# Query blocks for the score mix: the GpSimd queue issues whole second blocks three steps ahead, the SyncE queue takes the rest

## The chip, the cores and the metric

One core of a Trainium2 chip runs the whole program. The metric is the device time of one execution in microseconds (us); three runs of the kernel before gave 610.6, 612.25 and 614.14 us, so the median is 612.25 us. Five engines work side by side, each through its own instruction queue in order: TensorE (PE for its matmuls, PEld for the weight loads that go ahead of them), VectorE (DVE), ScalarE (ACT), GpSimd (POOL) and SyncE (SP). A DMA is issued by an instruction in the queue of SP, ACT or POOL, and lands later.

## The reference, cut to what matters

```python
scores = scale * q @ k^T                              # batch 2, heads 12, seq 448, head_dim 64
scores = einsum('bhij,hg->bgij', scores, w_pre)       # heads mixed before the softmax
attn   = softmax(scores)                              # with max subtracted and 1e-9 added to the sum
attn   = einsum('bhij,hg->bgij', attn, w_post)        # heads mixed after it
x      = (attn @ v) as [896, 768]
x      = ELU(x @ w1i) @ w1o                           # d_ff 2048
out    = silu(x @ w2i) @ w2o                          # d_ff 2048
```

## The kernel before, in words

The kernel has two parts. The first 165 us or so are the attention; after that come the two dense layers, in which TensorE runs one matmul behind the other.

The 896 query rows (2 batches of 448) are cut in two ways. For the scores they lie in seven tiles of 128 rows (`QTILES`, built from `CUTS`), and `qk_pair` makes the scores of one pair of heads of one tile; `qk_evac` copies them to an SBUF tile `s` with queries on the partitions. For the mix over heads the kernel needs heads on the partitions instead. So the queries are also cut in 90 blocks of 10 (`BI`), 45 for each batch, and a DMA moves each block from the `s` tile to the buffer `blk`: 10 queries x 12 heads make 120 rows of 448 scores. This DMA, line 167 in `move`, is what the change is about.

A step `s` (`NB` = 45 of them) works on two blocks, the first block `c = 0` and the second block `c = 1`. `blkb` holds three steps' blocks (`NBUF = 3`, slot `s % NBUF`). In a step:

- `premix(s)` (line 202) multiplies both blocks with `w_pre`: eight weight loads and eight matmuls, four for the first block and then four for the second.
- `rmax` (DVE, line 208), `exps` (ACT, line 220) and `recip` (DVE lines 228 and 229, then POOL line 233, which writes `krn`) make the softmax of step `s`.
- `postmix(s - 1)` (line 245) applies `w_post` and the softmax's divisor for the step before; `post_evac` (ACT line 133, DVE line 135) copies the result out.
- On the steps in `AV_AT` TensorE also multiplies with `v` (line 273), on those in `QK_AT` it makes a pair of heads of the next score tile (line 149). Tiles 2 to 6 are complete after steps 6, 16, 22, 28 and 34.
- From step 16 on the first weight chunks of the dense layers are loaded, scaled and split in between.

A block whose ten queries lie in one score tile in an even spacing is one DMA (one piece); a block that lies on an edge of a tile is two or three pieces. `BLOCKS[seq[2 * s + c]]` lists the pieces of block `c` of step `s`. Pieces of a first block that lie in the earlier tile are issued one step sooner (`early`).

`pooled(s, c)` decides the queue: POOL issues the second blocks of steps 3 to 31 (`POOLED = (3, 32)`), SP all others. `relayout(s, True)` issues what POOL has of step `s`, `relayout(s)` what SP has. `AHEAD = 2`: both are called two steps ahead, POOL's at the top of `step`, SP's near its end. In SP's queue loads from HBM stand between the blocks: queries, keys, values and weights. In POOL's queue the order through the steps is therefore: block of step `s + 2`, `krn` of step `s`, block of step `s + 3`, `krn` of step `s + 1`, and so on. The order of the whole program is written out by hand (`manual_schedule`); each instruction waits on semaphores for what it reads and for the buffer that it overwrites.

Of the kernel before, what the change touches and what calls it, by code (L numbers as in the profile page):

```python
# [30 lines left out]
NBUF = 3  # L31
NE = 3
LEAD = 5
POOLED = (3, 32)
TURN = (29, 35, 41)
LATE = (35, 37, 41)
KO = (0, 2, 4, 1, 3, 5)
AHEAD = 2
# [19 lines left out]
def spread():  # L58

    tiles, blocks = [], {}  # L60
    for T, segs in enumerate(CUTS):
        of = [None] * P
        for b, q, n, whole, left, right in segs:
            k = -(-q // BI)
            for j, aps in [(k - 1, left)] + [(k + x, a) for x, a in enumerate(whole)] + [(k + n, right)]:
                i = q % BI if aps is left else 0
                for r, d, m in aps:
                    blocks.setdefault((b, j), []).append((T, r, d, m, i))
                    for x in range(m):
                        of[r + d * x] = (b, j * BI + i + x)  # L70
                    i += m
        tiles.append((of, [x[0] for x in segs]))
    return tiles, blocks


QTILES, BLOCKS = spread()
# [3 lines left out]
def attn_moe_moe(ctx: ExitStack, tc: tile.TileContext, q, k, v, w_pre, w_post, w1i, w1o, w2i, w2o, out):  # L80
# [81 lines left out]
    seq = [(b, n) for b in range(B) for n in range(KB)]  # L162
    NB = len(seq) // 2

    def move(s, c, piece):
        T, r, d, m, i = piece
        (nc.gpsimd if pooled(s, c) else nc.sync).dma_start(blkb[4 + H * i:4 + H * (i + m), s % NBUF, c], smap[T][r:r + d * (m - 1) + 1:d])

    def pooled(s, c):
        return c == 1 and POOLED[0] <= s < POOLED[1]  # L170

    def early(n):
        x = BLOCKS[seq[n]]
        return [y for y in x if n % 2 == 0 and y[0] < x[-1][0]]

    def relayout(s, pool=False):

        if s >= NB:
            return
        for c in range(2):  # L180
            if pooled(s, c) != pool:
                continue
            gone = early(2 * s + c)
            for piece in BLOCKS[seq[2 * s + c]]:
                if piece not in gone:
                    move(s, c, piece)
        if s + 1 < NB and not pool:
            for piece in early(2 * s + 2):
                move(s + 1, 0, piece)
# [6 lines left out]
    def premix(s):  # L196
        tags = (("pre1", "pre2"), ("av", "pre0"), ("qk1", "pre0"))[s % 2 + (s % 2 and s > NB - 9)]
        pre[s] = [ps.tile([P, S], F32, name=f"pre{s}_{r}", tag=tags[r], bufs=1) for r in range(2)]
        for c in range(2):
            for r in range(2):  # L200
                o = slice(HS * r, HS * r + (HS if r == 0 else BW))
                nc.tensor.matmul(pre[s][r][HS * c:HS * c + HS], kpre[o], blkb[o, s % NBUF, c], start=True, stop=True, tile_position=(HS * r, HS * c))  # L202

    def rmax(s):
        n = prow(s)
        nmx[s] = ap_.tile([P, 2], F32, name=f"nmx{s}", tag="nmx", bufs=3)
        for r in range(2):
            nc.vector.tensor_reduce(nmx[s][:n, r:r + 1], pre[s][r][:n], axis=AX.X, op=ALU.max, negate=True)  # L208
            if r == 0 and s - 1 in LATE:
                recip(s - 1)  # L210

    def exps(s, between=None):
        n = prow(s)
        pexp[s] = []
        sums[s] = ap_.tile([P, 2], F32, name=f"sum{s}", tag="sum", bufs=3)
        for r in range(2):
            if r and between:
                between()
            t = ap_.tile([P, S], F32, name=f"pe{s}_{r}", tag="pe", bufs=4)
            nc.scalar.activation(t[:n], pre[s][r][:n], AF.Exp, bias=nmx[s][:n, r:r + 1], scale=1.0, accum_out=sums[s][:n, r:r + 1])  # L220
            pexp[s].append(t)
        del pre[s], nmx[s]

    def recip(s):

        n = prow(s)
        z = sums.pop(s)
        nc.vector.tensor_scalar(z[:n], z[:n], 1e-9, None, op0=ALU.add)
        nc.vector.reciprocal(z[:n], z[:n])  # L229
        kr[s] = []  # L230
        for r in range(2):
            t = ap_.tile([P, H, 5], F32, name=f"krn{s}_{r}", tag="krn", bufs=4)
            nc.gpsimd.tensor_scalar(t[:n], kps[:n], z[:n, r:r + 1], None, op0=ALU.mult)  # L233
            kr[s].append(t)
# [3 lines left out]
    def postmix(s):  # L238

        w = pst[s] = [x.rearrange("p (r c) -> p r c", r=2) for x in pbank]  # L240
        for r, m in [(0, m) for m in range(6)] + [(0, 6), (1, 6)] + [(1, m) for m in range(6)]:
            u, j = r if m == 6 else m % 2, m // 2
            for c in range(2):
                o = slice(HS * c, HS * c + BW)
                nc.tensor.matmul(w[c][HS * u:HS * u + HS, r, j * BW:(j + 1) * BW], pexp[s][r][o, m * HS:(m + 1) * HS], kr[s][r][o].rearrange("p h i -> p (h i)"), start=True, stop=True, tile_position=(HS * c, HS * u))  # L245
        del pexp[s], kr[s]
# [4 lines left out]
    def post_evac(s):  # L251
        for c, w in enumerate(pst.pop(s)):
            b, n = seq[2 * s + c]
            T, n = 4 * b + n // 12, n % 12
            if T not in amap:
                amap[T] = ap_.tile([P, 4 * H, TI], F32, name=f"a{T}", tag="a", bufs=2)
            o = amap[T][:NV, :, n * BI:(n + 1) * BI].rearrange("p x (r i) -> p r x i", r=2)
            evac((nc.scalar, nc.vector)[c], o, w[:NV].rearrange("p r (x i) -> p r x i", i=5))
# [70 lines left out]
    def at(d, step, f):  # L329
        d.setdefault(int(step), []).append(f)  # L330
# [20 lines left out]
    def run(d, s):  # L351
        for f in d.get(s, []):
            f()

    def step(s):
        relayout(s + AHEAD, True)
        if s < NB:
            premix(s)
        if s - 1 in LATE:
            rmax(s)  # L360
        run(X_AT, s)
        run(QK_AT, s)
        run(F_AT, s)
        if 0 <= s - 1 < NB:
            postmix(s - 1)
        if s < NB:
            if s - 1 not in LATE:
                rmax(s)
            exps(s, (lambda: post_evac(s - 1)) if s in TURN else None)
        two = s in X_AT  # L370
        if two:
            run(B_AT, s)
            if s < NB:
                recip(s)
            av_evac()
            av_split()
            run(A_AT, s)
        qk_evac(0)
        qk_evac(1)
        if 0 <= s - 1 < NB and s not in TURN:  # L380
            post_evac(s - 1)
        if not two:
            run(B_AT, s)
            if s < NB and s not in LATE:
                recip(s)
        relayout(s + AHEAD)
        run(D_AT, s)
        run(M_AT, s)
# [616 lines left out]
    for n in range(O1 + 8, I2):  # L1005
# [4 lines left out]
        if po:  # L1010
            c = chunks[n][2]
# [122 lines left out]
    while n < NCH:  # L1134
        c, k = chunks[n][2:]
# [95 lines left out]
```

## Time and profile before

| | |
|---|---|
| median of three runs | 612.25 us (610.6 to 614.14) |
| the profiled execution | 610.48 us |
| its span (first to last instruction) | 608.7 us |
| granted TensorE clock | 0.999 of full speed |
| PE busy | 592.4 us, 97% of the span |
| DVE busy | 452.6 us, 74% |
| ACT busy | 373.0 us, 61% |
| POOL busy | 83.9 us, 14%, all in the first 175 us |
| `blk<-s` DMAs | 69 issued by SP, 35 by POOL |

"Busy" is counted by engine over the whole span. The chain of waits is the work that ended last, followed back from the last instruction to what released it each time. A number in square brackets behind an instruction is the time for which its engine stood idle before it, with what ended the wait.

### The profile page before, as it was taken

What the parts mean: (1) busy time and instruction counts of PE and PEld (TensorE: products, weight loads), DVE (VectorE), ACT (ScalarE), POOL (GpSimd) and SP (SyncE); (2) the same over time, 40 slices, a digit from 0 to 9 for tenths busy, and PEclk for the clock granted to TensorE, in tenths of its full rate; (3) what the DMA queues carried; (4) which work ended last, traced back from release to release, by engine and by line L of the source; (5) the groups of instructions that cost most, each with busy time, mean ns of one, the idle gap of its engine ahead of it and who ended that gap; (6) DMA issues with size and microseconds to landing.
All of it is one profiled execution on the core that took longest, in us unless ns stands there. A gap on an engine that the chain in (4) does not pass through costs nothing.

```text
span 608.7 us, 15033 instructions
## 1 busy us (share of the span) xinstructions
PE 592.4 (97%) x6139; PEld 505.3 (83%) x6139; DVE 452.6 (74%) x755; ACT 373.0 (61%) x686; POOL 83.9 (14%) x152
## 2 busy tenths in 40 slices
PE   9788999999999999999999999999999999999997
PEld 3445656566799899999999999999999999999996
DVE  4765778798747999886776675599888888966642
ACT  4665777787837966758783553377676666533321
POOL 1444434446560000000000000000000000000000
PEclk9999999999999999999999999999999999999999
DMA  6755677663503253332435323434343323453601
GB/s 222 227 190 171 198 201 198 201 203 139 185 3 103 83 167 115 115 119 88 130 104 148 95 87 107 153 105 155 116 144 105 114 86 112 139 166 113 219 5 60
DMA packets 36385, 82.04 MB, mean 135 GB/s; under 512 B 5197, under 2 KB 15845, under 8 KB 36317
## 3 DMA queue, kind: packets, MB, share of 16 engines
q1 hardware_dynamic: 31549, 70.63, 36.2%
q0 software_dynamic: 2608, 6.25, 3.5%
q10 hardware_dynamic: 2160, 4.21, 2.3%
q8 instruction: 48, 0.79, 0.6%
q14 instruction: 20, 0.16, 0.1%
HBM read 59.05 MB, written 2.75 MB: 102 GB/s over the span
## 4 chain that ended last, share of the span: by engine, by line
PE 87%; DMA 6%; DVE 3%; ACT 3%; issue 1%; POOL 1%; DVEq 0%; ACTq 0%; POOLq 0%
PE po L557 31%; PE b L820 28%; PE av L273 5%; DMA blk<-s 5%; PE pre L202 4%; PE pq L149 4%; PE post L245 4%; PE q L1080 4%; PE ph L543 3%; PE po L1080 2%; DVE nmx L208 1%; PE post L543 1%; ACT pe L220 1%; POOL krn L233 1%; PE warm L313 1%
## 5 line engine op out<-in xcount | busy, mean ns | idle before, releaser
L820 PE MATMUL b<-x,we 128*128 128x448 f32 x360 | 93.7, 363 | 0.0
L220 ACT ACTIVATE pe<-pre,nmx 124x448 f32<-124x448 f32 x90 | 56.4, 631 | 34.5 <-DVE nmx L208 30.2
L820 PEld LDWEIGHTS b<-x,we 128*128 128x128 f32 x360 | 67.5, 188 | 4.6 <-DVE we L563 0.2
L820 PE MATMUL b<-rr,we 128*128 128x448 f32 x288 | 69.5, 362 | 0.0
L772 ACT ACTIVATE wr<-wr 128x768 f32<-128x768 f32 (+1 forms) x61 | 52.8, 865 | 18.3 <-DMA wr<-in_w1o_dram 8.5
L245 PEld LDWEIGHTS post<-krn,pe 60*64 60x64 f32 x2520 | 45.5, 135 | 21.6 <-issue 10.3
L208 DVE TENSOR_REDUCE nmx<-pre 124x1 f32<-124x448 f32 x90 | 51.9, 615 | 13.9 <-PE pre L202 12.6
L557 PE MATMUL po<-ge,we 128*128 128x448 f32 x216 | 60.3, 362 | 0.0
L557 PE MATMUL po<-gs,we 128*128 128x448 f32 x216 | 59.9, 362 | 0.0
L768 DVE SCALAR_TENSOR_TENSOR wc<-wr,wc 128x768 int32<-128x768 int32 (+1 forms) x62 | 56.2, 907 | 3.9 <-ACT wr L772 0.4
L202 PE MATMUL pre<-blk,kpre 64*64 64x448 f32 x360 | 50.3, 542 | 8.2 <-DMA blk<-s 8.0
L820 PEld LDWEIGHTS b<-rr,we 128*128 128x128 f32 x288 | 54.1, 188 | 3.5
L233 POOL TENSOR_SCALAR krn<-kps,sum 124x60 f32<-124x60 f32 x90 | 38.2, 432 | 91.0 <-DVE sum L229 61.9
L557 PE MATMUL po<-x,we 128*128 128x448 f32 x192 | 50.1, 362 | 0.0
L273 PEld LDWEIGHTS av<-a,v 128*64 128x64 f32 x768 | 36.9, 137 | 15.6 <-ACT pe L220 5.6
L514 DVE TENSOR_TENSOR we<-wc,we 128x640 fp32r<-128x640 f32 (+1 forms) x31 | 26.7, 862 | 30.7 <-ACT we L505 30.7
L245 PE MATMUL post<-krn,pe 60*64 60x60 f32 x2520 | 47.1, 219 | 2.0 <-POOL krn L233 1.7
L557 PE MATMUL po<-ta,we 128*128 128x448 f32 x168 | 44.8, 362 | 0.0
L149 PE MATMUL pq<-kt,qt 64*64 64x448 f32 x336 | 42.1, 562 | 1.0 <-ACT s L156 1.0
L557 PEld LDWEIGHTS po<-ge,we 128*128 128x128 f32 x216 | 40.6, 188 | 2.7
L557 PEld LDWEIGHTS po<-gs,we 128*128 128x128 f32 x216 | 40.5, 188 | 2.7
L752 ACT CAST we<-wc 128x768 fp32r<-128x768 f32 (+1 forms) x34 | 28.2, 830 | 22.4 <-DVE wc L768 8.9
(155 smaller groups left out, 1114.5 us busy)
## 6 DMA issues: line engine op xcount, KB each, us to landing
wr<-in_w2i_dram SPq DMA_DIRECT2D x32, 384.0 KB
wr<-in_w1i_dram SPq DMA_DIRECT2D x29, 384.0 KB
blk<-s SPq DMA_DIRECT2D x53, 210.0 KB
wr<-in_w1o_dram SPq DMA_DIRECT2D x24, 384.0 KB
wr<-in_w2o_dram SPq DMA_DIRECT2D x24, 384.0 KB
blk<-s POOLq DMA_DIRECT2D x24, 210.0 KB, 4.5
wr<-in_w1o_dram SPq DMA_DIRECT2D x12, 256.0 KB
wr<-in_w2o_dram SPq DMA_DIRECT2D x12, 256.0 KB
```

The lines of the kernel that those rows point to most:

```text
L149: nc.tensor.matmul(pq[e][HS * c:HS * c + HS], qT[T][half, p, HS * c:HS * c + HS], kT[p][half, bs[c % len(bs)]], start=True, stop=True, til ...
L202: nc.tensor.matmul(pre[s][r][HS * c:HS * c + HS], kpre[o], blkb[o, s % NBUF, c], start=True, stop=True, tile_position=(HS * r, HS * c))
L208: nc.vector.tensor_reduce(nmx[s][:n, r:r + 1], pre[s][r][:n], axis=AX.X, op=ALU.max, negate=True)
L220: nc.scalar.activation(t[:n], pre[s][r][:n], AF.Exp, bias=nmx[s][:n, r:r + 1], scale=1.0, accum_out=sums[s][:n, r:r + 1])
L233: nc.gpsimd.tensor_scalar(t[:n], kps[:n], z[:n, r:r + 1], None, op0=ALU.mult)
L245: nc.tensor.matmul(w[c][HS * u:HS * u + HS, r, j * BW:(j + 1) * BW], pexp[s][r][o, m * HS:(m + 1) * HS], kr[s][r][o].rearrange("p h i -> p ...
L273: nc.tensor.matmul(avt[T][e * D:(e + 1) * D, p % 2, :m], vall[b][:NV, h, j], amap[T][:NV, j * H + h, :m], start=j == 0, stop=j == 3, tile_ ...
L557: nc.tensor.matmul(po, wt[:, kk * P:(kk + 1) * P], g_op(moe, k0 + kk, hf, gi), start=(k0 == 0 and n_ == 0), stop=(k0 + kn == (KF, KS)[moe] ...
L768: nc.vector.scalar_tensor_tensor(cc, r[:, :, 1], 3, cc, op0=ALU.logical_shift_left, op1=ALU.bitwise_or)
L772: nc.scalar.activation(hf, hf, AF.Prelu, scale=2.0 ** -112, alpha=2.0 ** 32)
L820: nc.tensor.matmul(o, wt[:, u * KH + i * P:u * KH + (i + 1) * P], X[x, i][:, xi], start=start and n_ == 0, stop=n_ == 8, skip_group_check= ...
L1080: nc.tensor.matmul(o, wt[:, u * KH + i * P:u * KH + (i + 1) * P], t[i][:, xi] if x == "B22" else t[:, i, xi], start=start and n_ == 0, sto ...
```

## The change

```diff
+APART = (19, 25)
...
     def pooled(s, c):
-        return c == 1 and POOLED[0] <= s < POOLED[1]
+        return c == 1 and POOLED[0] <= s < POOLED[1] and s not in APART and len(BLOCKS[seq[2 * s + 1]]) == 1
...
     def step(s):
-        relayout(s + AHEAD, True)
         if s < NB:
             premix(s)
+        relayout(s + NBUF, True)
```

POOL now issues the second block of step `s + 3` right behind `premix(s)`, which is the last reader of that slot of `blkb`; before, it issued the block of step `s + 2` ahead of `premix(s)`. The second blocks that are made of several pieces (steps 5, 12, 18, 25 and 31) and that of step 19 go to SP, which still issues two steps ahead: 12 of the 35 DMAs of POOL become DMAs of SP, each behind the first block of its step. The second blocks of steps 19 and 25 are the ones whose score tile is completed only in the step in which POOL would issue them three steps ahead (16 and 22). `AHEAD` keeps its value for SP and for the start. Nothing is computed otherwise.

## Rows read from the trace of the kernel before

**Rows 1.** The page, busy time of TensorE's matmuls and its share.

```profile
PE 592.4 (97%) x6139; PEld 505.3 (83%) x6139; DVE 452.6 (74%) x755; ACT 373.0 (61%) x686; POOL 83.9 (14%) x152
```

**Rows 2.** Chain that ended last, in order of time: start us, us, what.

```profile
18.84 6.17 DMA blk<-s
...
29.61 5.97 DMA blk<-s
...
49.27 6.31 DMA blk<-s
...
78.26 6.55 DMA blk<-s
...
108.61 5.71 DMA blk<-s
...
211.35 64.13 PE b L820 x318
```

**Rows 3.** Waits of PEld, 14 to 185 us: total us, times, longest.

```profile
PEld pre L202 <- DMA blk<-s: 13.3, 8, 2.9
```

**Rows 4.** Timeline, PEld, first mixes: start, us, instruction, [idle before <-releaser].

```profile
16.22 0.19 PEld L202 LDWEIGHTS pre<-blk,kpre 64*64 64x64 f32 x4 [0.62 <-DMA blk<-s]
...
25.05 0.14 PEld L202 LDWEIGHTS pre<-blk,kpre 64*64 64x64 f32 x2 [2.60 <-DMA blk<-s]
...
27.37 0.20 PEld L202 LDWEIGHTS pre<-blk,kpre 64*64 64x64 f32 x4
...
35.63 0.14 PEld L202 LDWEIGHTS pre<-blk,kpre 64*64 64x64 f32 x2 [2.48 <-DMA blk<-s]
...
55.62 0.38 PEld L202 LDWEIGHTS pre<-blk,kpre 64*64 64x64 f32 x4 [2.89 <-DMA blk<-s]
...
69.38 0.19 PEld L202 LDWEIGHTS pre<-blk,kpre 64*64 64x64 f32 x4 [0.19 <-DMA blk<-s]
...
84.86 0.19 PEld L202 LDWEIGHTS pre<-blk,kpre 64*64 64x64 f32 x4 [2.11 <-DMA blk<-s]
...
114.37 0.19 PEld L202 LDWEIGHTS pre<-blk,kpre 64*64 64x64 f32 x4 [1.77 <-DMA blk<-s]
```

**Rows 5.** Timeline of POOL alone: its queue in order.

```profile
18.05 0.84 POOL L233 TENSOR_SCALAR krn<-kps,sum 124x60 f32<-124x60 f32 x2 [14.99 <-ACT s L156]
18.84 0.84 POOL L167 DMA_DIRECT2D blk<-s  x1
...
24.55 1.20 POOL L167 DMA_DIRECT2D blk<-s  x2
...
74.58 0.68 POOL L167 DMA_DIRECT2D blk<-s  x1 [0.60 <-ACT a L133]
...
104.64 0.64 POOL L167 DMA_DIRECT2D blk<-s  x1
```

**Rows 6.** The tile blk: its DMAs' issue times (min/median/max ns) and landing.

```profile
L167 SPq DMA_DIRECT2D blk<-s x69: 673/773/1078, 10.7 to 157.7; - x69
...
DMA to landing us min/median/max: 2.6/4.4/6.6
```

**Rows 7.** Timeline of all engines: DMA issues in SP's queue.

```profile
13.33 2.40 SPq L167 DMA_DIRECT2D blk<-s  x3
...
45.27 1.63 SPq L167 DMA_DIRECT2D blk<-s  x2
...
46.95 1.28 SPq L125 DMA_DIRECT2D kt<-in_k_dram  x1
```

**Rows 8.** Timeline of DVE: row maximum of step 3.

```profile
26.05 1.16 DVE L208 TENSOR_REDUCE nmx<-pre 124x1 f32<-124x448 f32 x2 [2.50 <-PE pre L202]
```

**Rows 9.** Stretches: start:end, length, busy us of each engine, clock, DMA share, GB/s.

```profile
75.00:95.00 20.00, 18.67 (x464) 12.00 (x460) 15.42 (x37) 15.14 (x40) 7.53 (x16) 1.00 0.71 188
95.00:125.00 30.00, 29.00 (x800) 19.14 (x796) 24.34 (x58) 22.64 (x59) 12.75 (x26) 1.00 0.71 210
```

**Rows 10.** Waits of PEld from 160 us to the end.

```profile
PEld b L820 <- DVE we L563: 0.8, 3, 0.4
```

## The prediction

> **What bounds the kernel now.** I start with the page: PE is busy for 592.4 of 608.7 us [rows 1], so some 16 us are open to a change that only moves transfers. Where they lie is told by the chain that ended last, read in order of time [rows 2]. From 211 us on it is PE alone, in pieces of tens of us. In the attention it is broken five times by the same thing, a DMA `blk<-s` of 5.7 to 6.6 us, and each starts where POOL issues one. The waits of PEld [rows 3] say what that costs: before the first mix it stood 13.3 us for `blk` in eight waits. The timeline gives seven of the eight one by one [rows 4]; the eighth, in the start, is another 0.62 like the one at 16.22. Five are long and all five stand in front of the *second* block of a step (3, 6, 12, 20, 28): the first block's weight loads had run.
>
> The cause stands in POOL's queue [rows 5]: krn at 18.05, then the block at 18.84, which lands at 25.01 (18.84 + 6.17) [rows 2] while PE wants it at 25.05 - 2.60 = 22.45. That block (of step 3) could be issued no sooner, because krn of step 0 stands ahead of it in the queue, waiting for step 0's softmax. Landing takes 2.6 to 6.6 us from issue [rows 6], and a block issued behind krn(s-1) for step s+2 has some 4 to 6 us.
>
> **The change, part by part.**
>
> *The lead.* In POOL's queue the order was krn(s-1), block(s+2), krn(s); it becomes krn(s-1), block(s+3), krn(s). So a block keeps its place behind the same krn but is one step further ahead: block n goes out when block n-1 went out before. The new wait, for `premix(s)` to be done with the slot, delays nobody: behind it on POOL stands krn(s), which needs `premix(s)` itself by way of rmax and exps. Now the five places:
> - Step 3. There is no krn ahead any more; it is issued after `premix(0)`, around 15.5. With the worst landing of 6.6 [rows 6] it is there at 22.1, wanted at 22.45. Gain 2.60.
> - Step 6 takes the place at 24.55 [rows 5]. With the steps before it 2.60 sooner it is wanted at 35.63 - 2.48 - 2.60 = 30.55; it lands between 27.2 and 31.2 by the bounds of rows 6. I take the upper half, which just does. Gain 2.48, at worst 1.9.
> - Step 12 goes to SP (below). Gain 2.89.
> - Step 20 takes the place at 74.58 instead of 78.26; wanted at 84.86 - 2.11 = 82.75, 8.2 us later. Gain 2.11.
> - Step 28 takes 104.64 instead of 108.61; wanted at 114.37 - 1.77 = 112.60, 8.0 us later. Gain 1.77.
> - The small wait of 0.19 at 69.38 (step 16) goes too. The two of 0.62 in the start are SP's and stay.
>
> What is late next: step 4's block takes the place at 18.84, where a block landed at 25.01. It was wanted at 27.37 [rows 4], now at 27.37 - 2.60 = 24.77. So I charge 0.25; at worst (6.6) 0.7, at best nothing.
>
> *The six blocks on SP* (steps 5, 12, 18, 19, 25, 31; 12 DMAs of 0.77 us issue each [rows 6], 9.3 us in SP's queue). The tight one is step 12. SP issues its first block in two pieces at 45.27 to 46.90 [rows 7]; the second follows in two more, to 48.4. An SP block issued at 13.33 in an empty stretch let its weight load start at 16.22 [rows 4, 7], 2.9 us later. From 47.7 (start of the last piece) that gives 50.6, against 55.62 - 2.89 = 52.73 wanted. With the worst landing of any block, 6.6, it would be 54.3 and the gain 1.3 instead of 2.89. I take 2.9 us, the nearest row in kind, and keep 1.6 us as the other end. Behind it the key load at 46.95 slides by 1.5 us; its pair of heads is made steps later. The other five blocks come out in SP's queue about as early as they did in POOL's, or earlier: no krn stands ahead of them. A price for the extra DMAs on SP from the side of gain: POOL's own issues, 0.65 us each, fall away, but nobody waits for POOL there, so zero.
>
> The landings in rows 6 are those of POOL's blocks alone; no row shows an SP block landing under load. The Trainium skill ("DMA: Bandwidth & Descriptors", Queues, rings and completion order) says that each DMA engine takes turns between the queues that have work. By this rule a block moved from POOL's queue to SP's loses its own turn and stands behind what SP queued before it; if that cost the step 12 block the whole range of rows 6 the sum would be 10.2 instead of 11.8.
>
> *Does the gain reach the end?* The waits idled the others as well: DVE stood 2.50 us before the row maximum of step 3 for the same block [rows 8]. In the stretch 75 to 95 DVE was busy 15.42 of 20 us, ACT 15.14, in 95 to 125 it was 24.34 and 22.64 of 30 [rows 9]. Without the waits of 2.11 and 1.77 the busier one, DVE, stands at 15.42/17.89 and 24.34/28.23, 86% both, so PE stays the limit. DMA at 0.71 would go to 0.71 x 20/17.89 = 0.79. After 160 us the longest total wait of PEld for another engine is 0.8 us [rows 10]; the dense layers start when attention is done, and the whole shift reaches the end.
>
> **Sum.** 2.60 + 2.48 + 2.89 + 2.11 + 1.77 + 0.19 - 0.25 = 11.8 us. The profiled execution (span 608.7, with 1.8 us around it 610.48) becomes 598.7. It was 1.77 us under the median of its three runs; from the median, 612.25 - 11.8 = 600.4, which I predict. Bounds of the unknowns: less 0.45 (step 4), 0.6 (step 6) and 1.6 (step 12) gives 9.1 gained, 603.1. Above: 0.25 more, 12.1, so 600.2; with the scatter of the runs shown, -1.7 and +1.9, the forecast's own range is 598.4 to 605.
>
> **Rivals.**
> - *First blocks become the last to land.* SP's first blocks stay two steps ahead, now with 12 more DMAs among them and the same bytes in less time (DMA share 0.79). For it: step 4's and 6's margins are below 1 us, DMA runs at 0.71 already. Against: no row of before shows PE waiting for a first block after the start (the five long waits and the 0.19 are all for second blocks) [rows 3, 4]. If the waits come back at half their size, the gain is half: 5.9 us, 606.3.
> - *The waits only hide another chain.* DVE and ACT in order would take the time back as waits of PE on krn and the copies. The whole gain would need DVE at about 100% where I find 86%. Against it speaks the idle time before DVE's row maximum. Time: 612.
> - *Slower: SP's queue falls behind in every even step.* The place is the first block of steps 6 to 28, twelve even steps, which SP issues two steps ahead. If extra pieces and HBM loads ahead of it make it late by more than 11.8/12 = 0.98 us in each, the change is a loss; at 1.3 us each it costs 15.6 against 11.8, 616. For it: a block's landing spreads by 4 us [rows 6]. Against: the extra work is six blocks in 29 steps, not twelve, and SP idles between issues.
> - *It does not do what it says:* if POOL's block waited for something beyond `premix(s)`, such as the scores of a later tile, it would go out where it does now, and the second blocks are as late as before: 612, within the bound. The row at 74.58 shows such a wait of 0.60 us for tile 3, small because tile 3 is done by then.
>
> **How the numbers follow.** Forecast 0.66, half the gain 0.19, no change 0.09 (two rivals together), slower 0.06. The range 597.0 to 606.5 takes in the forecast's own and the half gain, leaving 0.15 above it; it begins 1.4 below the forecast's own since the sum leaves out that weight loads restart slowly behind a wait (0.38 us for four at 55.62, 0.20 at 27.37 [rows 4]: 0.18 each, 0.9 in five). Half a percent, 3.1 us, is about what a measurement of this kernel can tell from no change: faster 0.85, same 0.09, slower 0.06.
>
> **What would show it.** In the profile after, PEld's wait for `blk` falls from 13.3 to about 1.5 to 2 us; the chain has no `DMA blk<-s` at steps 12, 20 and 28; POOL shows a block right behind the first mix of step 0, near 15.5; the first dense matmuls start some 12 us sooner, and from there to the end it lasts as long as before. Step 12 is wrong if its second block still holds PEld; the queue argument is wrong if PEld's waits for `blk` stand in front of first blocks; the prediction is wrong if PEld's waits for `blk` go and the time comes back as waits on krn, ACT or DVE.

## The result, and the profile after

The changed kernel took 604.0 us, median of 4 runs (602.38 to 605.2), against 612.25 before. The ratio is 0.9862 with an interval of 0.9815 to 0.9909, so 8.4 us faster (5.6 to 11.3). A second set of 6 runs on another occasion gave 0.9884 [0.985, 0.9919], 7.0 us by the medians. Here and below, medians and ratios leave out the few executions that took some 2% longer than the others of their kernel. The profiled execution has a span of 601.7 us, 7.0 less than before. The forecast was 600.4 with a range of 597.0 to 606.5: sign and range hold, but of the 11.8 us of the sum some 7 to 8 came.

The page of the changed kernel, busy time by engine and one DMA queue (packets, MB, share of the engines' time), answers to [rows 1]:

```profile
PE 590.0 (98%) x6139; PEld 505.8 (84%) x6139; DVE 451.8 (75%) x755; ACT 373.5 (62%) x686; POOL 77.1 (13%) x140
...
q8 instruction: 48, 0.79, 0.6%
```

The chain that ended last, changed kernel, in order of time (start us, us, what), answers to [rows 2]:

```profile
16.48 7.12 DMA blk<-s
...
28.26 8.40 DMA blk<-s
...
76.56 0.50 PE post L246 x33
77.06 1.81 issue
78.87 0.51 PE post L246 x20
```

Three of the five long transfers of before (at 49.27, 78.26 and 108.61) are gone from the chain, as forecast. Two are left, and they are longer than any of before (7.12 and 8.40 us; the worst was 6.55). The one at 16.48 is issued by SP: it is the first block of step 3. And there is a new piece, 1.81 us of `issue`: TensorE stood in the middle of a mix, and no semaphore or other engine in the profile ended that wait. PEld's waits in the changed kernel from 13 to 185 us (total us, times, longest), beside [rows 3]:

```profile
PEld post L246 <- issue: 12.4, 49, 1.9
...
PEld pre L203 <- DMA blk<-s: 4.7, 6, 1.5
```

The same view of the kernel before has this row for `issue`:

```profile
PEld post L245 <- issue: 10.3, 48, 0.2
```

So the wait for `blk` went from 13.3 to 4.7, not to 1.5 to 2; and the wait on `issue` grew by 2.1 us, with its longest going from 0.2 to 1.9. The timeline of PEld, changed kernel (start, us, instruction, idle before and its releaser), to be held against [rows 4]:

```profile
23.64 0.21 PEld L203 LDWEIGHTS pre<-blk,kpre 64*64 64x64 f32 x8 [1.17 <-DMA blk<-s]
...
26.51 0.21 PEld L203 LDWEIGHTS pre<-blk,kpre 64*64 64x64 f32 x8 [0.46 <-DMA blk<-s]
...
32.27 0.19 PEld L203 LDWEIGHTS pre<-blk,kpre 60*64 60x64 f32 x3 [0.38 <-DMA blk<-s]
...
36.71 0.19 PEld L203 LDWEIGHTS pre<-blk,kpre 64*64 64x64 f32 x4 [1.51 <-DMA blk<-s]
...
50.75 0.22 PEld L203 LDWEIGHTS pre<-blk,kpre 64*64 64x64 f32 x8
...
78.87 0.38 PEld L246 LDWEIGHTS post<-krn,pe 60*64 60x64 f32 x20 [1.94 <-issue]
...
106.86 0.21 PEld L203 LDWEIGHTS pre<-blk,kpre 64*64 64x64 f32 x8
```

At 50.75 (step 12) and 106.86 (step 28) the first mix's loads run through as one group of eight, where before the second four stood behind a wait of 2.89 and 1.77. At 23.64 (step 3) and 26.51 (step 4) the wait now stands in front of the whole group of eight, and at 32.27 (step 6) behind the first two loads of eight: it is the *first* block, SP's, that is late. At 36.71 (step 7) a second block is late, one that was in time before.

POOL's timeline, changed kernel, beside [rows 5]:

```profile
16.30 0.79 POOL L168 DMA_DIRECT2D blk<-s  x1 [13.25 <-PE pq L150]
18.12 0.85 POOL L234 TENSOR_SCALAR krn<-kps,sum 124x60 f32<-124x60 f32 x2 [1.02 <-ACT s L157]
18.91 0.65 POOL L168 DMA_DIRECT2D blk<-s  x1
...
25.01 0.65 POOL L168 DMA_DIRECT2D blk<-s  x1 [0.36 <-PE pre L203]
...
28.26 0.64 POOL L168 DMA_DIRECT2D blk<-s  x1
```

The order is as the change has it: a block stands ahead of krn of step 0, at 16.30 (15.5 had been expected; the row puts the end of its wait down to score matmuls, `pq`). The block issued at 28.26 is step 7's, and its landing is the 8.40 us of the chain. The tile `blk`, changed kernel, beside [rows 6]:

```profile
DMA to landing us min/median/max: 3.2/5.7/8.4
```

This row knows POOL's blocks alone, 35 DMAs before and 23 now. For the 23 that POOL issues in both kernels the least rose from 2.6 to 3.2, the median from 4.4 to 5.7 and the longest from 6.6 to 8.4 us; block by block, 19 landed later and 4 sooner. In the start the second blocks of steps 3 and 6 took about as long as before (6.1 both, against 6.2 and 6.0), those of steps 4, 7, 8 and 9 took 7.0, 8.4, 7.2 and 7.5 against 5.4, 4.1, 4.4 and 3.2. What the queues carry shows in the stretch that holds steps 0 to 9 (start:end, length, busy us of PE, PEld, DVE, ACT and POOL, granted clock, DMA share, GB/s), kernel before and then changed kernel:

```profile
13.50:45.00 31.50, 25.72 (x622) 13.46 (x616) 21.78 (x53) 20.05 (x53) 12.72 (x26) 1.00 0.66 211
```

```profile
13.50:45.00 31.50, 27.99 (x687) 15.71 (x680) 23.50 (x56) 20.88 (x57) 12.71 (x26) 1.00 0.80 228
```

DMA share rises from 0.66 to 0.80 while the rate rises only from 211 to 228 GB/s: for the same bytes the engines are busy longer. Where the 7.0 us are can be read from the starts of the first mix in each step (first weight load, from both timelines):

```
step              3      4      6      7      9     12     13     17     19     20     21     28     29     44    end
before        22.26  27.21  32.95  37.79  44.26  52.49  60.06  73.63  80.23  82.55  89.11 112.40 118.20 164.51  608.7
after         23.64  26.51  31.70  34.95  42.54  50.75  55.03  68.22  74.82  79.16  83.48 106.86 110.71 157.02  601.7
difference    +1.38  -0.70  -1.25  -2.84  -1.72  -1.74  -5.03  -5.41  -5.41  -3.39  -5.63  -5.54  -7.49  -7.49   -7.0
```

### The profile page after: what moved, and what is told of

Read it like the earlier page. It is cut to its first block, busy times and chain, and to the rows that moved or that the text cites. A ratio compares the mean times of both kernels' runs of the same rounds, so it can differ in the third digit from the quotient of the medians.

```text
span 601.7 us, 15018 instructions
## 1 busy us (share of the span) xinstructions
PE 590.0 (98%) x6139; PEld 505.8 (84%) x6139; DVE 451.8 (75%) x755; ACT 373.5 (62%) x686; POOL 77.1 (13%) x140
## 4 chain that ended last, share of the span: by engine, by line
PE 90%; ACT 3%; DMA 3%; DVE 2%; issue 1%; POOL 1%; ACTq 0%; DVEq 0%; POOLq 0%
PE po L558 31%; PE b L821 28%; PE av L274 5%; PE pq L150 5%; PE pre L203 5%; PE post L246 5%; PE q L1081 4%; PE ph L544 3%; DMA blk<-s 3%; PE po L1081 2%; ACT pe L221 1%; PE post L544 1%; DVE nmx L209 1%; PE warm L314 1%; POOL krn L234 1%
## 5 line engine op out<-in xcount | busy, mean ns | idle before, releaser
L203 PE MATMUL pre<-blk,kpre 64*64 64x448 f32 x360 | 47.5, 543 | 2.9 <-DMA blk<-s 2.1
```

## The experiments

All edits are against the changed kernel unless said otherwise; ratios are to the kernel before in the same set, with their 95% interval.

### The changed kernel once more, and its two parts apart

**The changed kernel, a second profile.** No edit. It asks which rows of the first profile repeat.

> The changed kernel once more, as the yardstick for the next three. Its first profile shows TensorE standing 1.8 us at 77 to 79 us, in the middle of a postmix, for nothing that the trace names (issue). If that is a lasting effect of the change (instructions fetched late, because the DMA engines are loaded there), it stands again within a few us of 77 us and the time is again 0.986 of before. If it was chance, it is gone or elsewhere and the profiled span is about 2 us shorter, near 599.8 us.

604.35 us, ratio 0.9884 [0.985, 0.9919]; the profiled span is 604.2, not 599.8. The gains of steps 12 and 28 repeat (3.30 and 1.95 us between step starts). That of step 20 does not: its first block is late, and behind it comes a wait for ACT. The long `issue` does not stand at 77 us, but there are others. PEld's timeline of this run:

```profile
44.59 0.61 PEld L246 LDWEIGHTS post<-krn,pe 60*64 60x64 f32 x36 [1.35 <-issue]
...
58.87 0.13 PEld L246 LDWEIGHTS post<-krn,pe 60*64 60x64 f32 x1 [1.18 <-issue]
...
79.80 0.21 PEld L203 LDWEIGHTS pre<-blk,kpre 64*64 64x64 f32 x8 [0.95 <-DMA blk<-s]
...
85.62 0.21 PEld L203 LDWEIGHTS pre<-blk,kpre 64*64 64x64 f32 x8 [1.45 <-ACT wr L472]
```

So stalls on `issue` belong to the kernel, but their places move from run to run. Each profile here is of one execution, and differences between single profiles have to be read with that in mind.

**The lead alone.** The six blocks issued in pieces or named in `APART` go back to POOL, two steps ahead (behind the first mix of the step, not ahead of it as in the kernel before):

```diff
-        return c == 1 and POOLED[0] <= s < POOLED[1] and s not in APART and len(BLOCKS[seq[2 * s + 1]]) == 1
+        return c == 1 and POOLED[0] <= s < POOLED[1]
+    def whole(s):
+        return s not in APART and len(BLOCKS[seq[2 * s + 1]]) == 1
...
-        relayout(s + NBUF, True)
+        if s + AHEAD < NB and not whole(s + AHEAD):
+            relayout(s + AHEAD, True)
+        if s + NBUF < NB and whole(s + NBUF):
+            relayout(s + NBUF, True)
```

> The lead alone: whole second blocks go out three steps ahead on POOL, the six others stay on POOL two steps ahead. Theory (the lead does most of the gain, SP's part removes step 12's wait alone): the wait of 2.9 us in front of step 12's second block is back, time 3 us above the changed kernel, ratio to before near 0.991. Rival (the 12 DMAs more on SP cost in the first blocks what they give at step 12): no slower than the changed kernel, ratio 0.986 or lower.

607.59 us, 0.9949 [0.992, 0.9977]. The wait of step 12 is back, and the kernel is 3.2 us behind the whole change:

```profile
54.01 0.45 PEld L206 LDWEIGHTS pre<-blk,kpre 64*64 64x64 f32 x4 [3.03 <-DMA blk<-s]
```

**SP's part alone.** The blocks that stay on POOL are issued two steps ahead as before, ahead of the first mix:

```diff
     def step(s):
+        relayout(s + AHEAD, True)
         if s < NB:
             premix(s)
-        relayout(s + NBUF, True)
```

> SP's part alone: the six blocks on SP, POOL's whole blocks still two steps ahead. Theory: step 12's wait of 2.9 us goes, those of steps 3, 6, 20 and 28 (2.6, 2.5, 2.1, 1.8 us) stay, time 3 us under before, ratio 0.995. Rival (POOL's queue without the six blocks and their waits is enough): the waits at 20 and 28 fall below 1 us too and the ratio is below 0.99.

611.33 us, 0.9993 [0.996, 1.0027]: no gain, where 0.995 was expected. In its profile the wait of step 12 is gone as well, but the others are larger than before (steps 3, 6 and 20, which were 2.60, 2.48 and 2.11 in [rows 4]); step 1's is 2.42 in place of 0.62, step 28's 1.09 in place of 1.77, and steps 9 and 24 have new ones (1.08 and 0.41):

```profile
25.77 0.14 PEld L203 LDWEIGHTS pre<-blk,kpre 64*64 64x64 f32 x2 [3.01 <-DMA blk<-s]
...
37.08 0.14 PEld L203 LDWEIGHTS pre<-blk,kpre 64*64 64x64 f32 x2 [3.21 <-DMA blk<-s]
...
86.05 0.29 PEld L203 LDWEIGHTS pre<-blk,kpre 64*64 64x64 f32 x4 [2.76 <-DMA blk<-s]
```

By the medians the parts do not add: 3.7 and 0.0 us alone, 7.0 together. But this profile is of one of the slower executions (614.26 us), and TensorE's granted clock fell in it twice, behind the waits of 3.21 and 2.76. The stretch behind the second (start:end, length, busy us, clock, DMA share, GB/s, as above):

```profile
86.00:88.00 2.00, 1.95 (x8) 0.56 (x10) 0.17 (x1) 0.00 (x0) 0.04 (x1) 0.52 0.77 191
```

The mean granted clock of an execution tells which ones had such a stretch: it is 0.999 or 1.000 in the eight profiles of this document without one, and 0.991 to 0.997 in the six with one or two. The four of the twelve in which it was 0.999 or more have a median of 607.9 us, the other eight one of 612.7. In the same set the kernel before has 611.1 at 0.999 or more, the lead alone 607.0, the whole change 604.35. At the high clock the parts are thus worth some 4.1 and 3.2 us, and the whole 6.8: they nearly add, and the 3 us that had been expected of SP's part are there. This picks executions after the fact, and few of them, so it is a strong hint and no proof; but the missing gain of SP's part can't be put down to the blocks alone.

### Is it the load on the queues in the first 45 us?

**Batch 0's v loads later.** They go from steps 0, 1, 3, 5 to 4, 5, 7, 9, out of the way of the first blocks:

```diff
-    for g, st in enumerate((0, 1, 3, 5)):
+    for g, st in enumerate((4, 5, 7, 9)):
```

> The changed kernel with the four loads of batch 0's values (384 KB each) issued at steps 4, 5, 7 and 9 instead of 0, 1, 3 and 5; they are read from step 8 on. Theory (the first 45 us are bound by the DMA engines: blocks issued sooner share them with these loads and land no sooner): PEld's waits for blk before step 9 fall from 4 us to under 1.5, step 8 starts at 36 to 37 us instead of 38.1, time 1.5 to 2.5 us under the changed kernel, ratio near 0.982. Rival (DVE and ACT in order set the pace of the first steps as soon as blocks are there): the waits for blk fall but step 8 starts within 0.7 us of 38.1 and the time is that of the changed kernel.

604.76 us, 0.9898 [0.9865, 0.9931]: no gain. PEld's timeline shows why. The waits for `blk` in steps 3 to 8 are gone, but one of 2.90 stands at step 1 with a stretch of low clock behind it (0.60 from 19 to 21 us), one of 0.91 at step 20, and stalls on `issue` have come in:

```profile
18.35 0.20 PEld L203 LDWEIGHTS pre<-blk,kpre 64*64 64x64 f32 x4 [2.90 <-DMA blk<-s]
...
59.95 0.13 PEld L246 LDWEIGHTS post<-krn,pe 60*64 60x64 f32 x1 [1.44 <-issue]
```

The wait at step 1 need not come from the moved loads: the run with eight loads more, below, is the changed kernel up to step 13 and has one of 2.08 there.

**The lead only from step 9 on.** POOL's blocks of steps 3 to 8 are issued as before the change; step 5's stays with SP:

```diff
+        if s + AHEAD < 9:
+            relayout(s + AHEAD, True)
         if s < NB:
             premix(s)
-        relayout(s + NBUF, True)
+        if s + NBUF >= 9:
+            relayout(s + NBUF, True)
```

> The changed kernel with the lead taken back for the first steps: POOL's second blocks of steps 3 to 8 go out two steps ahead, at the place they had before; from step 9 on three steps ahead; SP keeps its six. Theory A (the early lead gave the 2.5 to 3 us by which step 8 starts sooner in the two profiles): time 2 to 3 us over the changed kernel, ratio 0.992. Theory B (in the first 45 us the DMA engines are full whichever way blocks are issued, so the early lead gave nothing that lasts): within 0.7 us of the changed kernel, ratio 0.986 to 0.990.

606.31 us, 0.9908 [0.9881, 0.9936], 2.0 us behind the changed kernel by the medians (604.35) and 1.5 by the ratios: the lead in the start is worth about that, not the 4.83 us of the forecast's terms for steps 3, 6 and 4. The intervals of the two overlap, so the size is rough; the rows are plain. The waits of before are back at steps 3 and 6:

```profile
25.68 0.14 PEld L203 LDWEIGHTS pre<-blk,kpre 64*64 64x64 f32 x2 [2.53 <-DMA blk<-s]
...
36.34 0.14 PEld L203 LDWEIGHTS pre<-blk,kpre 64*64 64x64 f32 x2 [2.56 <-DMA blk<-s]
```

### What TensorE waits for when it waits for `issue`

The queue `q8 instruction` in the page gives a hint: 48 packets, 0.79 MB, so 16 KB each. TensorE's 6139 matmuls and 6139 weight loads make 12278 instructions, and 0.79 MB / 12278 is 64 B. One packet is then 256 of TensorE's instructions. I counted TensorE's instructions in order (two for each weight load and its matmul, one for each of the 90 or so semaphore waits and drains in its queue) and noted the number behind which it stood longer than 0.3 us on `issue`. Left out are the 0.70 us that stand ahead of some of the AV multiplications in every kernel, and three waits that stand where the granted clock was 0.50 (0.50 us at 20.42 in v later; 0.50 at 38.95 and 1.39 ahead of an AV at 87.73 in SP's part alone):

```
kernel             stalls, us from 20 us on   behind instruction                 remainder by 256
before             0                          -                                  -
changed            2.29 in 2                  962 3265                           194 193
changed, again     3.18 in 3                  962 1473 2241                      194 193 193
lead alone         1.22 in 3                  962 3266 3522                      194 194 194
SP's part alone    0                          -                                  -
v later            3.73 in 4                  962 1730 2241 4289                 194 194 193 193
lead from step 9   1.56 in 1                  4289                               193
```

All 13 lie at 193 or 194 by 256, which chance would not do: they are stalls at a boundary of two pieces of TensorE's program. The packet records give the mechanism. In the kernel before TensorE crosses a boundary at 77.85, the next packet runs from 79.13 to 80.15 and is needed at 82.22, 2.1 us later. In the changed kernel it crosses at 72.34, the packet runs from 76.26 to 77.22, so it starts 3.9 us behind the crossing, and TensorE goes on at 78.87, 1.65 us behind the packet's end. In all 13 stalls TensorE goes on 1.3 to 1.8 us behind the packet's end, so of the 2.1 us of before only some 0.4 were in hand. A piece lasts some 3.5 to 6 us when TensorE runs without waits. That packets of TensorE's program sometimes start late is shown; why this one started 3.9 us behind the crossing is not. Up to 160 us the median start is 0.9 us behind the crossing in the kernel before and 1.2 in the changed one, and five packets of before start more than 2 us behind it (up to 3.2) without a stall.

The remaining experiments ask whether transfers in the way cause it.

**One quarter of batch 1's v nine steps later**, from step 18 (ahead of the stall at 77) to 27:

```diff
-        e, st = ((D_AT, 18), (A_AT, 24), (A_AT, 28), (A_AT, 32))[g]
+        e, st = ((D_AT, 27), (A_AT, 24), (A_AT, 28), (A_AT, 32))[g]
```

> The changed kernel with one load less in the crowded stretch: the first quarter of batch 1's values (384 KB) is issued by SP at step 27 instead of step 18; it is read from step 30 on. Theory (what is left of the gain is lost to loaded DMA engines, which deliver blocks and TensorE's own instruction pieces late): fewer waits between 66 and 85 us, time 0.5 to 2 us under the changed kernel, ratio to before 0.983 to 0.988. Rival (behind step 12 the DMAs have room, and the stalls come from elsewhere): the time of the changed kernel within 0.5 us, and stalls of issue stand there as before.

605.68 us, 0.9896 [0.9867, 0.9924]: no gain. The stall at 77 is not there, but the profile has five others, 6.18 us in all, at instructions 962, 1218, 4801, 5057 and 7873 (194 or 193 by 256 again). The first two, 2.14 and 1.55 us, stand ahead of step 9, where this kernel is still the changed one; it starts step 9 3.1 us later than the first profile did. A stretch of low clock behind the second stall has its part in that. So much can two executions of the same instructions differ.

**Eight loads more**, 384 KB each, of data that is there already, in steps 13 to 27:

```diff
+    for n, st in enumerate((13, 15, 17, 19, 21, 23, 25, 27)):
+        at(D_AT, st, lambda g=(2, 3)[n % 2 or n > 5]: load_v(1, g))
```

> The changed kernel with eight loads more: SP loads quarters 2 and 3 of batch 1's values (384 KB each, the same data to the same place) once more at steps 13, 15, 17, 19, 21, 23, 25 and 27. Theory (loaded DMA engines cost time, by late blocks and late instruction pieces): 3.1 MB at about 215 GB/s is 15 us of DMA time within some 60 us; TensorE's waits for blocks and for issue grow by 3 us or more and the time by 2 to 6 us, ratio 0.992 to 0.998. Rival (the lead of three steps covers it all): within 1 us of the changed kernel, ratio 0.986 to 0.990.

613.38 us, 1.0044 [1.0013, 1.0075]: 9 us behind the changed kernel by the medians, the whole gain and a little more, where at most 6 had been expected. Landing of `blk` in this run:

```profile
DMA to landing us min/median/max: 5.0/6.3/10.6
```

and PEld's timeline:

```profile
81.08 0.21 PEld L203 LDWEIGHTS pre<-blk,kpre 64*64 64x64 f32 x8 [2.69 <-DMA blk<-s]
...
110.28 1.47 PEld L246 LDWEIGHTS post<-krn,pe 60*64 60x64 f32 x51 [2.85 <-issue]
```

The stall of 2.85 stands at instruction 4545, 193 by 256. By the starts of the steps, this kernel is 3.5 us behind the changed one at step 21, and 5.9 more go between steps 26 and 29. The stall alone doesn't make 5.9. The windows of this run (columns as above) show what does:

```profile
109.00:111.00 2.00, 0.71 (x28) 0.72 (x31) 0.00 (x0) 0.00 (x0) 0.00 (x0) 0.62 0.77 194
111.00:113.00 2.00, 2.00 (x45) 1.50 (x43) 0.68 (x1) 0.93 (x2) 0.00 (x0) 0.50 0.60 181
113.00:115.00 2.00, 2.00 (x23) 1.24 (x19) 1.16 (x2) 0.80 (x4) 0.64 (x1) 0.50 0.81 237
```

Behind the stand TensorE's granted clock is 0.50, the lower of its two levels (1.2 GHz), for some 6 us. A short stand cost about as much again behind it. In the first profile of the changed kernel the clock stays at 1.00 behind 78.87, so this is no part of its 7.0 us. One rival stands: the added loads go through SP's own queue, ahead of its first blocks, and the wait of 2.69 at 81.08 is for a first block. That POOL's blocks land later too (median 6.3 in place of 5.7) speaks for the load on the engines; how the 9 us divide between the two was not tried.

**Both moves of v together** (batch 0's later and batch 1's quarter later), the two diffs above:

> Both moves of loads together: batch 0's four value loads at steps 4, 5, 7 and 9, batch 1's first at step 27. Theory (loaded DMA engines hold what is left of the gain): waits for blk before step 9 under 1.5 us, fewer stalls of issue at 66 to 85 us, time 1 to 3 us under the changed kernel, ratio 0.981 to 0.986. Rival (TensorE's instruction pieces and DVE's order take the place of each wait that goes): the time of the changed kernel within 0.7 us.

605.3 us, 0.9884 [0.9854, 0.9913]: no gain again. The waits for `blk` are down to 1.16 us from 20 us on, all at step 20's first block, and the stalls on `issue` are up to 5.97 in five. Step 9 starts 4.50 us sooner than in the kernel before, step 10, behind the first long stall, only 2.80:

```profile
42.78 0.61 PEld L246 LDWEIGHTS post<-krn,pe 60*64 60x64 f32 x36 [1.63 <-issue]
...
108.58 0.20 PEld L203 LDWEIGHTS pre<-blk,kpre 60*64 60x64 f32 x6 [1.62 <-issue]
```

In these runs the loads moved and the stalls came elsewhere. The rest takes loads away.

**No loads of batch 1's k and v** (2.95 MB less; batch 1 is computed with batch 0's), in the changed kernel and, as a control, in the one before:

```diff
-... kT[p][half, bs[c % len(bs)]] ...
+... kT[p][half, 0] ...
-... vall[b][:NV, h, j] ...
+... vall[0][:NV, h, j] ...
-        at(e, st, lambda p=p, e=e: load_k(1, p, nc.scalar if e is A_AT else nc.sync))
+        pass
-        at(e, st, lambda g=g, e=e: load_v(1, g, nc.scalar if e is A_AT else nc.sync))
+        pass
```

> The changed kernel without the loads of batch 1's keys and values (six of 224 KB and four of 384 KB, 2.95 MB between steps 8 and 32); batch 1 is computed with batch 0's keys and values, TensorE's instructions are the same in number and shape. It is the mirror of the eight loads more. Theory (loaded DMA engines deliver blocks and TensorE's instruction pieces late): stalls of issue over 0.3 us behind step 8 add up to less than 1 us, time 2 to 5 us under the changed kernel, ratio to before 0.979 to 0.985. Rival (TensorE outruns its instruction pieces at this pace whatever the DMA engines carry): the stalls stay at 2 to 5 us, ratio 0.986 to 0.990.

> The kernel before without the same ten loads (batch 1 computed with batch 0's keys and values), as the control. Theory (landing times grow with the load): its waits at steps 12, 20 and 28 shrink from 6.8 us together to 2 to 4 us and the time by 3 to 5 us, ratio 0.992 to 0.995, which is to be taken off the gain of the changed kernel without the loads. Rival (the waits come from POOL's place in its queue alone): the waits and the time stay, ratio 0.998 to 1.002.

602.73 us, 0.9835 [0.9809, 0.9861], and 608.44, 0.9919 [0.9893, 0.9945]; the change is worth 5.7 us at this load. In the control the waits of steps 12, 20 and 28 shrink from 6.8 us to 3.3 together, as the theory had it (0.83, none and 2.43), while new ones come in at steps 18 and 22 (1.50 and 0.57). The changed kernel has no stall on `issue` from step 8 on, where the loads are left out, but two ahead of it, where they are not:

```profile
34.32 0.13 PEld L203 LDWEIGHTS pre<-blk,kpre 64*64 64x64 f32 x2 [2.59 <-issue]
...
40.70 0.29 PEld L246 LDWEIGHTS post<-krn,pe 60*64 60x64 f32 x4 [1.29 <-issue]
```

and behind the second one the low clock again:

```profile
40.00:42.00 2.00, 1.30 (x13) 0.50 (x12) 0.73 (x2) 0.68 (x2) 0.00 (x0) 0.67 0.50 165
42.00:44.00 2.00, 2.00 (x18) 1.40 (x16) 1.32 (x3) 0.56 (x2) 1.44 (x3) 0.50 0.05 16
```

**Three of the four loads of batch 0's v left out too** (all heads read the first quarter), changed kernel and control:

```diff
+... vall[0][:NV, h % 3, j] ...
-    for g, st in enumerate((0, 1, 3, 5)):
+    for g, st in enumerate((3,)):
```

> The changed kernel without batch 1's keys and values and also without three of batch 0's four value loads (384 KB each, steps 0 to 5), one load at step 3 is left; all heads are multiplied with the first quarter of batch 0's values, TensorE's instructions are the same in number and shape. In the run without batch 1's loads the stalls at TensorE's instruction pieces were gone behind step 8 and stood at 2.6 and 1.3 us before it. Theory (they come from the load on the DMA engines): now they are gone there too (under 0.7 us in all), PEld's waits for blk between 20 and 45 us are under 1.5 us, time 2.5 to 4 us under that run, ratio to before 0.976 to 0.980. Rival (in the first steps TensorE outruns its pieces at any load): the stalls at 31 to 45 us stay over 2 us, ratio 0.982 to 0.986.

> The kernel before without the same thirteen loads, as the control. Without batch 1's loads it stood at 0.992. Theory (its waits come from POOL's place in the queue, load lengthens them): waits at steps 3 and 6 fall from 5.1 to 3 to 4.5 us, no stall at an instruction piece, ratio 0.988 to 0.991. If the load is all that held the forecast's 11.8 us back, the changed kernel without these loads lies 10 us or more under this one; if the forecast was too large of itself, 6 to 9 us.

600.23 us, 0.9808 [0.9786, 0.983], and 607.24, 0.9941 [0.9919, 0.9963]. In the changed kernel's early stretch, and the landing of `blk` there:

```profile
13.50:45.00 31.50, 29.39 (x767) 16.05 (x765) 24.86 (x59) 23.28 (x62) 13.85 (x29) 1.00 0.58 194
...
DMA to landing us min/median/max: 2.6/4.1/8.7
```

DMA share 0.58 in place of 0.80, PE busy 29.39 in place of 27.99, no wait for `blk` from 20 to 45 us and no stall on `issue`. The median landing is 4.1 us in place of 5.7. Step 8 starts 4.69 us sooner, and step 29 11.56 sooner, than in the kernel before *with all its loads*. That is close to the forecast's 4.83 and 11.8, but it does not confirm them, for the kernel before gains from the lost loads too: its step 8 starts 3.91 sooner, and against it the changed kernel is only 0.78 ahead there. Then comes one stall, at 109.52:

```profile
109.52 0.79 PEld L246 LDWEIGHTS post<-krn,pe 60*64 60x64 f32 x48 [1.16 <-issue]
```

Against its own control the change is worth 7.0 us by the medians. Of the two cases that had been set apart beforehand this is the second, "too large of itself"; but they left out that the control's waits for `blk` shrink as well (from 13.3 to 8.2), so that less is left to gain: the wait falls from 8.2 to 2.0 here. In that control the waits of steps 3 and 6 fall from 5.1 to 0.65, further than the theory had it. Its profile (611.92 us, the slowest of the ten counted) has one long stall on `issue` itself, with a stretch of low clock behind it:

```profile
112.53 0.30 PEld L202 LDWEIGHTS pre<-blk,kpre 60*64 60x64 f32 x6 [3.26 <-issue]
```

So such stalls are not the lead's alone, nor does taking load away exclude them; in this one profile there are none in the early stretch, and that is all these runs carry.

## Why the prediction was right, and where its sum was off

**What bounds the kernel: right.** Waits for second blocks, put there by POOL's queue, were the price. Those of steps 3, 6, 12, 20 and 28 are gone, and with either part taken back some of them return. But waits for first blocks have come in, 2.0 of the 4.7 us in the first profile. By the prediction's own signs that speaks against the queue argument where it happens, in the start and at step 20.

**The lead and SP's part from step 12 on: right for steps 12, 16 and 28, not for step 20.** From one step start to the next the changed kernel gained 3.29 at step 12 (2.89 priced), 0.38 at step 16 (0.19) and 1.95 at step 28 (1.77), and nearly the same in the second profile (3.30, 0.38, 1.95). The lead alone brings the wait of step 12 back, so that term is SP's part; SP's part alone leaves those of steps 3, 6 and 20, so these are the lead's. The prediction's remark on slow restarts, 0.18 us in each of five places, rests on one row: four loads take 0.38 us at 55.62, but 0.19 behind the waits of 2.11 and 1.77 [rows 4].

Step 20 was priced at 2.11. From the start of step 19 to that of step 21 the changed kernel gained 0.22 in the first profile and lost 0.30 in the second. With the second block in time, the first block of step 20 holds PEld: in the second profile the mix starts at 79.80, 0.95 us late, and SP had issued the block 7.5 us before:

```profile
72.28 0.80 SPq L168 DMA_DIRECT2D blk<-s  x1
```

The same wait stands at step 20 in seven of the other variants (0.70 to 1.16 us, and 2.69 with eight loads more), with the fewest loads too (0.83). In the first profile the stall at 77 stands ahead of it and gives the block that much more time, which is probably why no wait shows. Why this block takes so long is not shown.

**Step 12 on SP: right in that the mix doesn't wait.** I had put 2.9 us on a piece issued by SP and kept 6.6 as the other end. In the changed kernel SP issues the step's four pieces from 43.55 on and the mix at 50.75 doesn't wait:

```profile
43.55 3.21 SPq L168 DMA_DIRECT2D blk<-s  x4
```

The last piece goes out at 46.11, 1.6 us sooner than forecast, so it had 4.7 us to land; no run shows 2.9 us there. Nor was the row that gave 2.9 from "an empty stretch": from 13.3 to 16.3 us the DMA share of the kernel before is 0.68. With 6.6 us the mix would have waited. The rule of the Trainium skill that I weighed ("DMA: Bandwidth & Descriptors", Queues, rings and completion order) would have allowed a loss here; no run in which SP has the block shows one at step 12, with or without the lead. What it says of the queues' turns may be why first blocks, all SP's, are late in step 3: that is only argued.

**The step where the sum was off: it let a step start as soon as its second block had landed, and the sum priced no first block.** Steps 3, 6 and 4 together stood at 2.60 + 2.48 - 0.25 = 4.83. They brought 1.72 by step 9 (2.42 in the second profile). The second blocks of steps 3 and 6 did land within the bound of 2.6 to 6.6 us (6.1 both); step 4's took 7.0. What held step 3 was SP's first block: issued at 16.48, as before (16.39), it was needed no later than 22.26 in the kernel before and was there, and now it landed after 7.1 us, with POOL's block issued beside it at 16.30 in place of 18.84. Step 3 waits 1.17 for it; the first blocks of steps 4 and 6 are 0.46 and 0.38 late. The bound itself failed for step 7's second block (8.4 us, 1.51 late): it came from a trace in which these blocks were issued a step later. With batch 0's v loads out of the way and all loads still made (both moves of v), step 9 starts 4.50 sooner, near the 4.83; this is one profile, without a control, but it points to those loads as what the blocks met. The size by step 9 is rough in any case: up to step 8 four other profiles are of the same instructions, and their step 9 starts between 2.7 us sooner and 1.7 later than before; the two late ones have the long stalls at 962 and 1218. The rival of late first blocks was right in kind, in steps 3, 4, 6 and 20, though not in the size that I gave it.

**What the sum did not have: TensorE's own instructions.** I checked DVE, ACT and DMA as the next bound and found DVE at 86%. In the first profile PEld's waits for ACT grew from 14.9 to 17.6 us and those for krn fell from 9.6 to 7.6, so they took little. PE's supply of instructions took more: 2.0 us between the starts of steps 19 and 20 in the first profile, 3.18 us of stalls in the second. In the trace of before `issue` stands in front of the second mixes as 48 gaps of at most 0.2 us, so its rows gave no price; but the queue's row (48 packets for 12278 instructions) was on the page.

**The account** for the first profile, by step starts: 11.8, less 3.11 (4.83 - 1.72) in steps 3 to 9, plus 0.77 above the terms of steps 12, 16 and 28, less 1.89 at steps 19 and 20 (2.11 priced, 0.22 come, the stall at 77 among it), less 0.58 between the steps named and from step 44 to the end, is 6.99; measured 7.0. It says where the time went, and closes by the way it is made.

The dense layers do start sooner by the whole shift (-7.49 at step 44) and take as long as before but for 0.5 us. The rivals "another chain" and "doesn't do what it says" fall with the gain; "SP falls behind in every even step" falls with the step starts, which keep their distance from step 21 to 27 and from 29 to 44; step 20 alone behaves like it.

**Left open.** Why one packet of instructions starts 1 us and another 3.9 us after the boundary; which transfers stand ahead of it; why step 20's first block takes 7.5 us and more. No version with all its loads was faster than the changed kernel: v later and both moves together lie within its interval. In their profiles what they gain for `blk` comes back as stalls on `issue`.

## What to carry to other kernels

A landing time read from a trace belongs to that trace's load: before a transfer is moved up, look at what else moves in the stretch it moves into, and price the transfers already there as well as the one moved. Where an engine runs thousands of small instructions without a pause, its own program is a stream of transfers that needs a place too: read the instruction queue in the page, count the engine's instructions in one packet, and see how long they last against how late a packet can be. An experiment that moves a load shows little if the load only meets another victim; leaving it out tells more, if the result is held against a control that lost the same load. A transfer that is priced as the last to land has neighbours that are next: price the first block as well as the second. And where a kernel's executions differ in TensorE's granted clock, compare them at one clock before a cause is named.

## What the runs showed of the hardware that I had not expected

- TensorE's program came in 48 packets of 16 KB, 256 instructions each. The 13 stalls on `issue` in the table's seven profiles, and 17 more in the other seven, lay at the same two neighbouring remainders by 256. They cost 0.3 to 2.9 us, and 3.26 once in the control with the fewest loads. In the 13, TensorE went on 1.3 to 1.8 us behind the end of its packet.
- The same 23 blocks on POOL's queue landed in 2.6 to 6.6 us before (median 4.4), in 3.2 to 8.4 after (5.7) and in 5.0 to 10.6 with 3 MB more beside them (6.3).
- Behind a stand of 2.85 us (ending 110.28) and one of 1.29 us (ending 40.70, after other pauses) the granted clock was 0.50 for some 3 to 7 us; behind stands of 1.94 us (changed kernel, 78.87) and 2.89 us (before, 55.62) it stayed at 1.00. Six of the fourteen profiles have such a stretch in the attention, two of them two. What tells these cases apart was not tried. SP's part alone took 607.9 us (median of four) in executions with a mean clock of 0.999 or more and 612.7 (of eight) in the others.
